# Nine value loads of a decode kernel issued as three partition ranges each

## The chip, the core and the metric

The kernel runs on one NeuronCore of one Trainium2 chip. The metric is the device time of one execution in microseconds (us). All times of the profile come from one profiled execution; "the span" is the time from its first to its last instruction.

## The reference

One decode step of a transformer block with adaptive layer norm, for 8 sequences (one token each) of width 1024:

```python
mod = silu(c) @ w_mod                                # c [8,1024], w_mod [1024, 6*1024]
sa, ca, ga, sb, cb, gb = six parts of mod
h = layernorm(x) * (1 + ca) + sa
x = x + ga * attention(h)                            # 32 query heads, 4 key/value heads of 128
h = layernorm(x) * (1 + cb) + sb
x = x + gb * ((relu(h @ W_gate) * (h @ W_up)) @ W_down)     # width 3584

def attention(h):
    q = h @ wq                                       # [1024, 4096]
    for each sequence b and each key/value head g:   # 8 * 4 = 32 pairs, 8 query heads each
        p = softmax(q @ k_cache[b, g].T / sqrt(128)) # k_cache[b, g]: 8192 x 128, bf16
        o = p @ v_cache[b, g]                        # v_cache[b, g]: 8192 x 128, bf16
    return o @ wo                                    # [4096, 1024]
```

Nearly all bytes are weights and caches that are read once: 64 blocks of keys and values of 2 MB each, and the six weight matrices, 185.6 MB in all.

## The kernel before

**One stream of loads.** Everything that comes from memory passes through one SBUF tensor, `ring` (128 partitions of 11 x 8192 bf16 columns), in a fixed order that the list `stream` holds: 4 blocks of `w_mod` ("mod"), 4 of `A_wq`, then for each of the 32 pairs n a key block ("k", n) and two places later a value block ("v", n), with 4 blocks of `A_wo` in between, then `B_W_gate` and `B_W_up` in turn (4 each), and `B_W_down` in five parts (7, 7, 7, 5 and 2 of 28). There are 89 loads. A key or value block is 8192 columns wide: each of the 128 partitions receives one contiguous piece of 16 KB. A planner written out in the kernel gives each block its place in the ring (`place`) and lists the blocks whose place it takes over (`behind`).

**Who issues and who waits.** All 89 loads are issued by SyncE (line 507 in the profile, engine SP), in the order of `stream`; before each it waits until TensorE has used the blocks that lay there (`users`). Load i signals one of 24 semaphores, i mod 24, and the operation `o` of the load holds the value that tells of its landing (`o.semval`); a semaphore rises by 16 with each transfer. A matmul that reads a block waits for that value. The two small inputs `c` and `x` (8 partitions of 2 KB each) are loaded by ScalarE's queue, and the four parts of the output (8 partitions of 512 B each) leave by SyncE's and ScalarE's queues.

**What the engines do with it.** For pair n, TensorE transposes the key block in 64 tiles (`slot_transpose`, L279 in the profile), VectorE and ScalarE copy them out of PSUM in turn (`slot_evac`, `KT`), and TensorE forms the scores with the transposed tile as its weights. The softmax of pair n-1 (its maximum, the subtraction, Exp) and the product with the values of pair n-2 (`slot_pv`) are woven into the eight steps of pair n. The multiplication with `A_wo` follows by groups of eight pairs. After the attention come the second layer norm, the gate and up products (448 matmuls) and the down product (112 matmuls in five parts, one part for each load of `B_W_down`), two VectorE operations, and the output.

Of the kernel before, what the change touches and what calls it, by code (L numbers as in the profile page):

```python
# [124 lines left out]
def bass_adaLN_cond__gqa_block_cached__glu_gated_reglu__decode_kernel(  # L125
# [30 lines left out]
    NSEM = 24  # L156
# [4 lines left out]
    with ExitStack() as es:  # L161
# [83 lines left out]
        place = {}  # L245
# [3 lines left out]
        for i, (key, cols, src, shape) in enumerate(stream):  # L249
            if at + cols > RING:  # L250
                at = 0
            lo, hi = at, at + cols
            behind.append([k for l, h, k in held if l < hi and h > lo])
            held = [x for x in held if not (x[0] < hi and x[1] > lo)] + [(lo, hi, key)]
            place[key] = ring[:, lo:hi].rearrange("p (k n) -> p k n", n=shape[1])
            at = hi
        loads = {}
        users = {}
        for i, (key, cols, src, shape) in enumerate(stream):
            o = _Op("sp", None, 0)  # L260
            o.sem = rsem[i % NSEM]
            o.semval = 16 * (i // NSEM + 1)
            loads[key] = o

        def pe(fn, reads=(), writes=(), block=None, deps=()):
# [232 lines left out]
        for q in range(4):  # L498
            o = g.dma("sp" if q % 2 == 0 else "act", out.rearrange("b o d -> (b o) d")[:, 256 * q:256 * (q + 1)], outR[32 * q:32 * q + B, :],
                      osem[q], 16, reads=["outR"])  # L500
# [3 lines left out]
        head = []  # L504
        for i, (key, cols, src, shape) in enumerate(stream):
            o = loads[key]
            o.fn = (lambda e, key=key, src=src, o=o: e.dma_start(place[key], src).then_inc(o.sem, 16))  # L507
            o.deps = [users[k] for k in behind[i]]
            head.append(o)
        g.prog["sp"] = head + g.prog["sp"]  # L510
# [40 lines left out]
```

## Time and profile before

| what | value |
|---|---|
| median of 3 runs | 457.0 us (456.96 to 457.01) |
| the profiled execution: its own time | 457.03 us |
| the profiled execution: its span | 455.2 us |
| TensorE busy (PE) | 367.0 us, 81% of the span |
| VectorE busy (DVE) | 175.1 us, 38% |
| ScalarE busy (ACT) | 155.0 us, 34% |
| data moved by SyncE's and ScalarE's queue q1 | 185.61 MB in 17968 packets, 97.3% of the 16 DMA engines' time |
| mean granted TensorE clock | 0.773 of full speed |

PE is TensorE's matmuls, PEld its weight loads, SPq the sequencer of SyncE, on which DMAs are issued. A DMA is carried out by up to 16 DMA engines, each of which moves packets one after the other; in this kernel a packet is one contiguous piece, 16 KB for keys and values. Beside instructions, the trace holds the start, duration, size and queue of each DMA packet (not the number of the engine that moved it), and the time of each landing mark, that is of each step by which a DMA raises its semaphore.

### The profile page before, as it was taken

The numbers are of one execution on the slowest core, as the hardware profiler recorded it, in microseconds if no ns is written. First come the engines' busy times: TensorE is split into PE (matmuls) and PEld (weight loads), VectorE is DVE, ScalarE is ACT, GpSimd is POOL, SyncE is SP. The second block draws the span as 40 slices with busy tenths as digits, with TensorE's granted clock in tenths as the row PEclk, the third lists the DMA queues.
The fourth block names the chain that finished last, engine by engine and source line by source line (L and its number), as shares of the span: only waits on it lengthen the run. The fifth ranks groups of instructions, "written<-read, shape, count | busy, mean of one in ns | idle before, by whom it ended". The sixth has DMA issues, their size and how long they took to land.

```text
span 455.2 us, 16982 instructions
## 1 busy us (share of the span) xinstructions
PE 367.0 (81%) x8008; PEld 353.0 (78%) x8008; DVE 175.1 (38%) x422; ACT 155.0 (34%) x169; POOL 1.5 (0%) x11
## 2 busy tenths in 40 slices
PE   2425487988889999999888698899989999859983
PEld 1425387987888889898888698888889888849971
DVE  1001033455445544445555235544544355530000
ACT  3000045354445434444444234444543344410000
POOL 1000000000000000000000000000000000000000
PEclk9999996598779767768989558967887578855555
DMA  8999999999999999999999999999999999999982
GB/s 348 440 410 421 428 423 430 429 417 426 423 428 422 406 429 424 420 425 429 423 411 416 430 420 426 429 423 417 412 425 425 423 426 400 377 418 420 425 369 112
DMA packets 18101, 186.73 MB, mean 410 GB/s; under 512 B 1472, under 2 KB 1504, under 8 KB 7792
## 3 DMA queue, kind: packets, MB, share of 16 engines
q1 hardware_dynamic: 17968, 185.61, 97.3%
q8 instruction: 62, 1.02, 0.9%
q10 hardware_dynamic: 64, 0.04, 0.0%
q14 instruction: 7, 0.06, 0.0%
HBM read 185.63 MB, written 0.02 MB: 408 GB/s over the span
## 4 chain that ended last, share of the span: by engine, by line
PE 54%; DMA 22%; DVE 12%; SPq 5%; issue 4%; ACT 1%; DVEq 0%
PE PS L279 33%; PE PS L275 21%; DMA ring<-in_A_k_cache_dram 15%; DMA ring<-in_B_W_down_dram 7%; SPq L507 5%; DVE KT L283 5%; DVE mp L283 3%; DVE dg L283 2%; DVE nm L283 1%; ACT KT L286 1%; ACT pt L286 0%; DVE ssub L283 0%; ACT L286 0%; DVE rl L283 0%; DVE outR L283 0%
## 5 line engine op out<-in xcount | busy, mean ns | idle before, releaser
L279 PE MATMUL PS<-identb,ring 128*128 128x128 bf16 x2048 | 199.7, 256 | 7.6 <-DMA ring<-in_A_k_cache_dram 5.5
L286 ACT ACTIVATE KT<-PS 128x1024 bf16<-128x1024 bf16 x128 | 131.0, 1023 | 191.6 <-PE PS L279 170.4
L279 PEld LDWEIGHTS PS<-identb,ring 128*128 128x128 bf16 x2048 | 153.6, 115 | 10.0 <-DMA ring<-in_A_k_cache_dram 6.2
L283 DVE COPY KT<-PS 128x1024 bf16<-128x1024 bf16 x128 | 88.6, 692 | 154.6 <-PE PS L279 153.6
L275 PE MATMUL PS<-qT,KT 128*128 128x8 bf16 x2048 | 94.0, 169 | 0.1
L275 PEld LDWEIGHTS PS<-qT,KT 128*128 128x128 bf16 x2048 | 89.3, 104 | 0.2 <-ACT KT L286 0.2
L275 PE MATMUL PS<-pt,ring 128*128 128x8 bf16 x2048 | 87.9, 167 | 1.3 <-issue 1.2
L275 PEld LDWEIGHTS PS<-pt,ring 128*128 128x128 bf16 x2048 | 71.0, 99 | 1.8 <-issue 1.7
L275 PE MATMUL PS<-dg,ones 8*128 8x8 f32 x64 | 14.1, 290 | 24.9 <-DVE dg L283 24.9
L275 PEld LDWEIGHTS PS<-dg,ones 8*128 8x128 f32 x64 | 11.2, 217 | 27.8 <-DVE dg L283 27.8
L275 PEld LDWEIGHTS PS<-h2T,ring 128*128 128x128 bf16 x448 | 28.5, 162 | 0.4 <-issue 0.4
L275 PE MATMUL PS<-h2T,ring 128*128 128x8 bf16 x448 | 28.5, 204 | 0.0
L275 PE MATMUL PS<-siluT,ring 128*128 128x8 bf16 x384 | 10.9, 168 | 14.6 <-DMA ring<-in_w_mod_dram 14.6
L283 DVE TENSOR_TENSOR ssub<-PS,nb 128x512 f32<-128x512 f32 x32 | 22.1, 692 | 1.2
L275 PEld LDWEIGHTS PS<-siluT,ring 128*128 128x128 bf16 x384 | 10.8, 105 | 14.9 <-DMA ring<-in_w_mod_dram 14.9
L283 DVE TENSOR_REDUCE mp<-PS 128x8 f32<-128x512 f32 x32 | 21.8, 681 | 0.4 <-PE PS L275 0.4
L286 ACT ACTIVATE pt<-ssub 128x512 bf16<-128x512 f32 x32 | 19.9, 622 | 3.5 <-DVE ssub L283 3.5
L275 PE MATMUL PS<-pt,onesb 128*128 128x64 bf16 x256 | 17.1, 225 | 1.7 <-ACT pt L286 1.7
L275 PE MATMUL PS<-hT,ring 128*128 128x8 bf16 x256 | 7.5, 168 | 11.5 <-DMA ring<-in_A_wq_dram 11.5
L275 PEld LDWEIGHTS PS<-hT,ring 128*128 128x128 bf16 x256 | 7.1, 104 | 11.9 <-DMA ring<-in_A_wq_dram 11.9
L286 ACT ACTIVATE qT<-PS 128x256 bf16<-128x256 f32 x1 | 0.4, 383 | 43.7 <-PE PS L275 43.7
L275 PEld LDWEIGHTS PS<-pt,onesb 128*128 128x128 bf16 x256 | 13.0, 117 | 1.9 <-ACT pt L286 1.9
(64 smaller groups left out, 107.0 us busy)
## 6 DMA issues: line engine op xcount, KB each, us to landing
ring<-in_A_k_cache_dram SPq DMA_DIRECT2D x32, 2048.0 KB, 37.2
ring<-in_A_v_cache_dram SPq DMA_DIRECT2D x32, 2048.0 KB, 37.8
ring<-in_w_mod_dram SPq DMA_DIRECT2D x4, 3072.0 KB, 21.4
ring<-in_A_wq_dram SPq DMA_DIRECT2D x4, 2048.0 KB, 42.7
ring<-in_A_wo_dram SPq DMA_DIRECT2D x4, 2048.0 KB, 42.6
ring<-in_B_W_gate_dram SPq DMA_DIRECT2D x4, 1792.0 KB, 28.9
ring<-in_B_W_up_dram SPq DMA_DIRECT2D x4, 1792.0 KB, 27.1
ring<-in_B_W_down_dram SPq DMA_DIRECT2D x3, 1792.0 KB, 29.1
```

The lines of the kernel that those rows point to most:

```text
L275: return pe(lambda e: e.matmul(out_, lhsT, rhs, start=start, stop=stop, skip_group_check=True), reads, writes, block, deps)
L279: return pe(lambda e: e.matmul(out_, in_, ident, start=True, stop=True, is_transpose=True), reads, writes, block)
L283: return g.op("dve", lambda e: getattr(e, name)(*args, **kw), reads, writes)
L286: return g.op("act", lambda e: e.activation(*args, **kw), reads, writes)
L507: o.fn = (lambda e, key=key, src=src, o=o: e.dma_start(place[key], src).then_inc(o.sem, 16))
```

## The change

Nine value blocks, those with n mod 7 equal to 1 or 4 (n = 1, 4, 8, 11, 15, 18, 22, 25, 29), are loaded by three transfers each in place of one: partitions 0 to 111, then 112 to 119, then 120 to 127. The three go out one behind the other on SyncE's queue and raise the same semaphore, by 48 in all, and the values that later loads of that semaphore reach are counted up accordingly. The data, its place in the ring, the order of the stream and the work of the other engines stay as they were; SyncE issues 107 loads in place of 89.

```diff
@@ -254,12 +254,20 @@
+
+        def cuts(key):
+            if key[0] == "v" and key[1] % 7 in (1, 4):
+                return [(0, 112), (112, 120), (120, 128)]
+            return [(0, 128)]
+
         loads = {}
         users = {}
+        landed = [0] * NSEM
         for i, (key, cols, src, shape) in enumerate(stream):
             o = _Op("sp", None, 0)
             o.sem = rsem[i % NSEM]
-            o.semval = 16 * (i // NSEM + 1)
+            landed[i % NSEM] += 16 * len(cuts(key))
+            o.semval = landed[i % NSEM]
             loads[key] = o
@@ -504,7 +512,7 @@
         for i, (key, cols, src, shape) in enumerate(stream):
             o = loads[key]
-            o.fn = (lambda e, key=key, src=src, o=o: e.dma_start(place[key], src).then_inc(o.sem, 16))
+            o.fn = (lambda e, key=key, src=src, o=o: [e.dma_start(place[key][a:z], src[a:z]).then_inc(o.sem, 16) for a, z in cuts(key)])
             o.deps = [users[k] for k in behind[i]]
```

## The prediction

> **What bounds the kernel now.** I read the busy shares first, then the end of the chain of waits, then what TensorE waits for at the end, and last the landing marks of single loads. The page, with shares of the span, 40 slices of DMA, and the queues:
>
> ```profile
> PE 367.0 (81%) x8008; PEld 353.0 (78%) x8008; DVE 175.1 (38%) x422; ACT 155.0 (34%) x169; POOL 1.5 (0%) x11
> ...
> DMA  8999999999999999999999999999999999999982
> ...
> q1 hardware_dynamic: 17968, 185.61, 97.3%
> q8 instruction: 62, 1.02, 0.9%
> ```
>
> No compute engine is full, and the DMA engines are, from the first slice to the last but one. The chain in order of time (start, duration, what), after the attention:
>
> ```profile
> 403.25 1.84 PE PS L275 x64
> ...
> 415.50 2.15 SPq L507
> 417.66 0.04 issue
> 417.70 32.30 DMA ring<-in_B_W_down_dram
> 450.00 0.04 issue
> 450.05 1.87 PE PS L275 x25
> ```
>
> It ends in a load of `B_W_down`. The timeline of TensorE in that stretch, with its idle time and what ended it:
>
> ```profile
> 411.25 28.54 PE L275 MATMUL PS<-h2T,ring 128*128 128x8 bf16 x448
> 440.36 1.66 PE L275 MATMUL PS<-ring,hmT 128*8 128x256 bf16 x28 [0.57 <-DVE hmT L283]
> 442.70 1.66 PE L275 MATMUL PS<-ring,hmT 128*8 128x256 bf16 x28 [0.67 <-DMA ring<-in_B_W_down_dram]
> 446.97 1.67 PE L275 MATMUL PS<-ring,hmT 128*8 128x256 bf16 x28 [2.61 <-DMA ring<-in_B_W_down_dram]
> 450.05 1.83 PE L275 MATMUL PS<-ring,hmT 128*8 128x256 bf16 x28 [1.41 <-DMA ring<-in_B_W_down_dram]
> ```
>
> TensorE has caught up and waits for each part. The last part lands at 451.24, and the span ends 4.0 later. So the end is the last landing plus a fixed tail.
>
> A load has landed when the slowest of its 16 streams (one for each DMA engine) has delivered its eight pieces. The trace's landing marks show that the streams drift apart. The 16 marks of the first `w_mod` block lie within 0.49 us, those of v31 between 381.13 and 392.44 (11.3 us), and those of the last part of `B_W_down` in two groups: eight between 441.38 and 442.45, eight between 449.23 and 451.24. **Eight late streams set the end.**
>
> Why eight are late can be read from the packets. The 62 packets of queue q8 (instructions, 16 KB, 1.07 us each) go to eight streams in turn. Where the first one falls, the stream's next packet starts 0.98 us late and takes 1380 ns in place of 912: 1.45 us lost, and 1.50 at the second. 62 / 8 x 1.5 = 11.6 us, which is the spread of v31.
>
> **Part by part.** *Which streams get more.* The loads of `c` and `x`, 8 partitions each, leave nine marks: one step made at once, and one from each of eight streams. So an 8-partition transfer runs on eight streams with one piece each. A cut load thus puts two pieces on eight streams A, those that serve 8-partition transfers, beside their share of the 112. That share appears in no row. At one end, 112 is split evenly over 16, 7 pieces each: A moves 7 + 1 + 1 = 9 in place of 8, the other eight, B, move 7. At the other end it is 8 pieces on 14 streams: A then moves 10. I take 7, because all 128-piece loads of this trace are split evenly over 16 streams. By the Trainium skill ("DMA: Bandwidth & Descriptors", section on why a DMA increments its semaphore by 16) a transfer uses the largest number of engines up to 16 that divides its partitions, the lowest-numbered ones: 16 for 112, eight for 8. The nine marks agree for 8, no run here shows 112, and the sum would be the same.
>
> *What a piece costs.* Key and value loads land every 4.89 us on an undisturbed stream, 0.611 us per piece. A's streams each get nine pieces more: 9 x 0.611 = +5.5 us, and 18 more completion packets of 6 to 9 ns, +0.1. B's get 9 x 0.611 = 5.5 us less.
>
> *Are late streams in A?* This decides the sign. On a stream, a packet starts 3 to 4 ns before the previous one ends, so streams can be followed from packet to packet. I marked the eight streams that carry a 2 KB piece of `x` (A) and followed all 16. The first two instruction packets (16.34 and 29.91) fall on streams of B, the third and fourth (37.91 and 47.07) on streams of A, each within 1 ns of the place where that stream's next packet was due. From 89.89 on the order repeats on the same streams. And the stream that is last in the first block, 0.54 us behind the first and without a piece of `x`, never gets one and stays in the early group. So the late eight are mixed: at least two of them are in A. Two streams a nanosecond apart can be taken for each other, which is why this is not certain; I give it 9 in 10.
>
> *The sum.* A late stream of A ends 5.6 us later. The two that I identified got eight instruction packets each, like the six marks between 450.7 and 451.24, so if neither of them is the very last, 0.5 us less counts: +5.1 to +5.6, taken as +5.4. The last landing moves from 451.24 to 456.6, and the tail is the same. What B gains is worth nothing, since a load waits for its last stream. The profiled execution took 457.03 (span 455.2 and 1.8 around it), the median of the runs 457.0; so 457.0 + 5.4 = **462.4 us**.
>
> *Costed at nothing.* SyncE issues 18 more DMAs, 0.433 us each at the median, 7.8 us in all. Behind each cut load in its queue stands the next key load. The cover is the backlog of the late streams: the tightest, the first `B_W_up` load, is issued at 387.85 and is begun on the latest stream at 403.56, 15.7 us later. Without that cover each cut load would cost 0.87 us, 7.8 in all. The longest issues (20.6 us for one value load, where the SP queue is held back) come behind `A_wo`; they hold back loads that the late streams reach much later. TensorE waits for one value as before, on the attention's blocks a few us later. It is then ready for the down product at 440.4 and would wait 3.4 us more for its first part; this is the same delay and not a second one.
>
> **Rivals.** *Shorter, because late and B are the same.* Then the late streams lose 5.5 us of work and end at 445.7, and the early ones end at 442.45 + 5.6 = 448.05. The last landing comes 3.2 us sooner: **453.8 us**. TensorE, ready for the down product at 440.36 with 6.8 us of its matmuls to do, would be done at 447.2 and does not prevent it. For it: the two groups are eight and eight, and 9 x 2 x 0.611 = 11.0 us is just the spread. Against it: the packets as followed above. It decides from the point where no late stream carries `x`: 0.09.
>
> *Longer, because pieces collide.* In a 128-piece load each stream writes its own partitions. In a cut load a stream writes partitions that are another's otherwise, and eight streams write 8 neighbouring partitions at once. If two streams that write into the same group of partitions share its way in, each runs at half speed. With one other writer, the 18 extra pieces take 0.611 us more each: 11 us, 473.4 us. With two, 22 us, 484.4; with four, 44 us, 506. Against it: the pieces of `x` went to partitions 0 to 7 while the `w_mod` block was being written there, and all eight took 84 ns, the smallest time of a 2 KB packet of `A_wo`, and no `w_mod` packet beside them lengthened by over 40 ns. They are only 2 KB, and so I leave it 0.24. The Trainium skill ("SBUF — State Buffer", "Door 1: The DMA port swizzle") states that 128 partitions share 16 ports of about 27 GB/s, and by its table 112 to 119 lie on two of them, 120 to 127 on two others. It speaks against this change, and by it four extra writers meet the regular one on a port; a 16 KB piece in 0.611 us is 26.8 GB/s, so an estimate by that page is the last of these cases.
>
> *112 is split over 14 streams.* A gets two pieces more per cut load: +11 us, **468.1 us**; 0.05.
>
> *Nothing moves*, because the cuts end up as one transfer, or the wait at the end is covered by TensorE. Against it: the built kernel's SyncE program does hold the transfers of 112 and of 8 partitions, and TensorE waits 4.7 us for the down blocks: 457.0, 0.02.
>
> **How the numbers follow.** Forecast 0.60, collisions 0.24, 14 streams 0.05, shorter 0.09, nothing 0.02. The likeliest gives 462.4. A change of 0.2%, 0.9 us, is about what a measurement of this kernel can tell from none. Slower: 0.60 + 0.24 + 0.05 = 0.89; faster 0.09; same 0.02. Range: the likeliest case alone is 461.5 to 463.5. Left out at the bottom are the shorter case and no change (0.11); at the top collisions with more than two other writers (0.08): 459 to 484.
>
> **What would show it.** Right: the marks of the last load of `B_W_down` spread over 19 to 21 us in place of 9.9, its last one at about 456.6 on the span's clock, with the packets of a 16 KB piece still at 0.61 us, the cut loads leaving 16 + 9 + 9 marks, and TensorE's waits for the down blocks 3 to 5 us longer. Wrong: a spread under 7 us and an earlier end (late and B are the same); pieces of 1.2 us and more in and behind the cut loads (collisions); an extra delay of 1.2 us per cut load on eight streams with packets at 0.61 (14 streams). If packets, spread and last mark are as forecast but the end is not, the fixed tail was the mistake.

## The result, and the profile after

The changed kernel takes **570.5 us** (median of 4 runs, 564.8 to 571.2) where the kernel before takes 457.0 (456.96 to 457.03): 1.2456 times as long, 95% interval 1.2388 to 1.2524. The direction was the forecast one; the size was not: 113.5 us in place of 5.4, and outside the range of 459 to 484. The profiled execution took 571.2, its span 569.4.

The lines of the page of the changed kernel that answer to those shown of before (busy time and share; DMA and GB/s in 40 slices; the queues):

```profile
PE 404.1 (71%) x8008; PEld 387.2 (68%) x8008; DVE 175.1 (31%) x422; ACT 155.1 (27%) x169; POOL 1.5 (0%) x11
...
DMA  8999999999999999999969999999299999589980
GB/s 365 434 414 425 427 208 410 349 253 423 415 209 364 425 200 292 411 341 211 318 217 344 270 394 425 236 375 387 90 250 389 429 268 376 188 345 419 424 373 20
...
q1 hardware_dynamic: 18112, 185.61, 92.5%
q8 instruction: 62, 1.02, 0.8%
```

(The packets of q1 are SyncE's alone; ScalarE's few went by q10, which the table of before had put under q1.) The same bytes move, and the DMA engines still look full in nearly all slices. But the rate falls to about half wherever a cut load is under way: 208, 253, 209, 200 beside 425. **Busy engines at half the rate mean longer packets, not missing ones.** A stretch between cuts, one around the second cut (v4) and one behind it, from the windows of the changed kernel (the last two columns are DMA share and GB/s):

```profile
90.00:107.00 17.00, 14.16 (x256) 13.99 (x256) 6.37 (x16) 5.04 (x6) 0.00 (x0) 0.52 1.01 425
108.00:125.00 17.00, 12.40 (x244) 11.83 (x242) 5.96 (x15) 5.64 (x6) 0.00 (x0) 0.65 1.02 226
128.00:145.00 17.00, 14.92 (x288) 14.63 (x285) 6.14 (x14) 6.87 (x8) 0.00 (x0) 0.60 1.01 425
```

The first two stretches in the kernel before:

```profile
90.00:107.00 17.00, 15.02 (x358) 14.59 (x356) 9.63 (x24) 8.20 (x9) 0.00 (x0) 0.90 1.01 424
108.00:125.00 17.00, 14.75 (x324) 14.35 (x322) 8.46 (x20) 6.84 (x8) 0.00 (x0) 0.79 1.01 427
```

In the packets of the trace, a 16 KB piece takes 0.61 us between cuts, 0.8 to 1.4 in the 112 partitions of v1 and up to 2.8 at its end, where the two transfers of 8 follow. Over the whole execution their mean rises from 618 to 780 ns.

TensorE's wait for keys is the longest of its DMA waits in the changed kernel's list (us in total, times, longest):

```profile
PEld PS L287 <- DMA ring<-in_A_k_cache_dram: 77.1, 24, 11.4
PE PS L287 <- DMA ring<-in_A_k_cache_dram: 73.1, 22, 11.3
```

The same wait before:

```profile
PEld PS L279 <- DMA ring<-in_A_k_cache_dram: 6.2, 2, 3.6
```

The end itself is unchanged, as the timeline of TensorE shows: it waits for the down blocks just as long as before, only 114 us later.

```profile
556.84 1.67 PE L283 MATMUL PS<-ring,hmT 128*8 128x256 bf16 x28 [0.81 <-DMA ring<-in_B_W_down_dram]
561.12 1.66 PE L283 MATMUL PS<-ring,hmT 128*8 128x256 bf16 x28 [2.61 <-DMA ring<-in_B_W_down_dram]
564.19 1.84 PE L283 MATMUL PS<-ring,hmT 128*8 128x256 bf16 x28 [1.40 <-DMA ring<-in_B_W_down_dram]
```

How much each cut costs can be read from the last landing marks of the loads behind it, against the same loads before: 7.4 us for v1, then 10.7, 11.6, 15.0, 18.9, 12.5, 13.4, 11.8 and 12.8, together 114.1. The last mark of the last load moves from 451.24 to 565.39, which is the same 114.1. From v17 on a single stream is late, where eight were late before: of the 16 marks of k27, fifteen lie within 2.5 us and the last comes 15.3 us after the first.

### The profile page after: what moved, and what is told of

Same layout as the page of the kernel before. It is cut to its first block, busy times and chain, and to the rows that moved or that the text cites. A ratio compares the mean times of both kernels' runs of the same rounds, so it can differ in the third digit from the quotient of the medians.

```text
span 569.4 us, 17000 instructions
## 1 busy us (share of the span) xinstructions
PE 404.1 (71%) x8008; PEld 387.2 (68%) x8008; DVE 175.1 (31%) x422; ACT 155.1 (27%) x169; POOL 1.5 (0%) x11
## 4 chain that ended last, share of the span: by engine, by line
DMA 43%; PE 38%; DVE 6%; another core or an unknown queue 5%; SPq 4%; issue 3%; ACT 0%; DVEq 0%
DMA ring<-in_A_k_cache_dram 31%; PE PS L287 23%; PE PS L283 14%; DMA ring<-in_A_wq_dram 6%; DMA ring<-in_B_W_down_dram 6%; SPq L515 4%; DVE KT L291 3%; DVE mp L291 1%; DVE dg L291 1%; DVE nm L291 1%; DVE ssub L291 0%; DVE stat L291 0%; ACT pt L294 0%; DVE xcT L291 0%
## 5 line engine op out<-in xcount | busy, mean ns | idle before, releaser
L287 PE MATMUL PS<-identb,ring 128*128 128x128 bf16 x2048 | 229.4, 281 | 77.2 <-DMA ring<-in_A_k_cache_dram 73.1
L287 PEld LDWEIGHTS PS<-identb,ring 128*128 128x128 bf16 x2048 | 176.3, 127 | 84.4 <-DMA ring<-in_A_k_cache_dram 77.1
L294 ACT ACTIVATE KT<-PS 128x1024 bf16<-128x1024 bf16 x128 | 131.1, 1024 | 305.0 <-PE PS L287 220.5
L283 PE MATMUL PS<-qT,KT 128*128 128x8 bf16 x2048 | 97.7, 171 | 0.0
L283 PEld LDWEIGHTS PS<-qT,KT 128*128 128x128 bf16 x2048 | 97.0, 109 | 0.0
L283 PEld LDWEIGHTS PS<-pt,ring 128*128 128x128 bf16 x2048 | 72.6, 101 | 7.1 <-issue 7.0
L283 PE MATMUL PS<-dg,ones 8*128 8x8 f32 x64 | 15.8, 317 | 24.7 <-DVE dg L291 24.7
L283 PEld LDWEIGHTS PS<-dg,ones 8*128 8x128 f32 x64 | 12.8, 248 | 27.5 <-DVE dg L291 27.5
L283 PEld LDWEIGHTS PS<-hT,ring 128*128 128x128 bf16 x256 | 7.1, 104 | 11.9 <-DMA ring<-in_A_wq_dram 11.9
```

What stands on the lines that cost most here:

```text
L283: return pe(lambda e: e.matmul(out_, lhsT, rhs, start=start, stop=stop, skip_group_check=True), reads, writes, block, deps)
L287: return pe(lambda e: e.matmul(out_, in_, ident, start=True, stop=True, is_transpose=True), reads, writes, block)
L294: return g.op("act", lambda e: e.activation(*args, **kw), reads, writes)
```

## Experiments

Four theories were open. **W**: streams that write into the same small group of partitions share one way into SBUF (below, a "way"), and a transfer that has not all 128 partitions gives streams other partitions than their usual ones. **S**: the streams meet at the source in memory. **N**: more transfers, marks and issues cost time. **U**: it is the unequal work of the streams, dearer than the sum put it.

**Transfers alone.** A kernel without the computation; each group is issued at once and has landed before the next begins. The thirteen groups, with eight loads each (`rows` takes ranges of partitions; a triple holds the partitions written, the rows read and the columns; `ALL` is all 8192; the comments give the number of the group):

```python
phase(rows((0, 128)))                                       # 1
phase(rows((0, 112), (112, 120), (120, 128)))               # 2
phase(rows((0, 112), (112, 128)))                           # 3
phase(rows((0, 112)))                                       # 4
phase(rows((0, 64), (64, 128)))                             # 5
phase([(slice(0, 128), slice(0, 128), c) for c in ((0, 7168), (7168, 7680), (7680, 8192))])   # 6
phase(rows((112, 120)))                                     # 7
phase([(slice(0, 32, 4), slice(112, 120), ALL)])            # 8
phase([(slice(0, 8), slice(112, 120), ALL)])                # 9
phase([(slice(0, 2), slice(0, 2), ALL)])                    # 10
phase([(slice(0, 8, 4), slice(0, 2), ALL)])                 # 11
phase([(slice(0, 64, 32), slice(0, 2), ALL)])               # 12
phase([(slice(0, 128, 64), slice(0, 2), ALL)])              # 13
```

> Transfers alone: the whole computation is left out, the output is zeros. Thirteen groups of eight loads each, with 16 KB to a partition, on SyncE's queue; a group starts when the one before has landed. In order: 128 partitions whole; 112+8+8; 112+16; 112 alone; 64+64; 128 partitions cut by columns in 7/8, 1/16, 1/16; then transfers of 8 partitions into 112 to 119, into every fourth of 0 to 31, into 0 to 7, all three from the same source rows; then transfers of 2 partitions into 0 and 1, into 0 and 4, into 0 and 32, into 0 and 64, again from the same source rows. Theory W (streams that write into the same small group of partitions share one way in): whole 39 us; by columns 39 to 42; 112+8+8 two to three times as much, 80 to 130, 112+16 and 112 alone well over 45; 64+64 about twice, 75 to 85; eight partitions into 112 to 119 about four times as long as into every fourth (20 against 5 us), the same for 0 to 7; two partitions into 0 and 1 and into 0 and 32 twice as long as into 0 and 4 and 0 and 64 (10 against 5 us), if the groups are those of the prediction's page. Theory S (the streams meet at the source in memory): the three groups of 8 partitions are alike, the four of 2 partitions are alike, 64+64 is like whole. Theory N (the number of transfers and marks costs): by columns is as slow as 112+8+8, and 112 alone takes 7/8 of whole, 34 us.

Windows of this kernel, one for each of the groups 1 to 6, then 7 and 8, then 10 to 13 (the last column, GB/s, counts the time to the landing too):

```profile
0.00:42.80 42.80, 1.15 (x5) 1.00 0.94 392
43.30:124.10 80.80, 0.00 (x0) 1.00 0.90 208
124.60:192.20 67.60, 0.00 (x0) 1.00 0.97 248
192.70:250.20 57.50, 0.00 (x0) 1.00 0.97 255
250.70:332.00 81.30, 0.00 (x0) 1.00 0.98 206
332.60:375.20 42.60, 0.00 (x0) 1.00 0.98 394
375.70:396.60 20.90, 0.00 (x0) 1.00 0.44 50
397.10:404.90 7.80, 0.00 (x0) 1.00 0.38 134
...
426.00:437.30 11.30, 0.00 (x0) 1.00 0.11 23
437.80:445.20 7.40, 0.00 (x0) 1.00 0.10 35
446.00:456.90 10.90, 0.00 (x0) 1.00 0.11 24
457.60:464.90 7.30, 0.00 (x0) 1.00 0.11 36
```

From the first packet to the end of the last, by the trace's packets, with the median packet of 16 KB:

| group | us | GB/s | packet, ns |
|---|---|---|---|
| 1: whole | 40.6 | 413 | 611 |
| 2: 112+8+8 | 79.5 | 211 | 1107 |
| 3: 112+16 | 66.6 | 252 | 1024 |
| 4: 112 alone | 56.6 | 260 | 989 |
| 5: 64+64 | 79.6 | 211 | 1276 |
| 6: by columns | 41.7 | 402 | (14 KB and 1 KB) |
| 7: 8 into 112 to 119 | 19.0 | 55 | 2407 |
| 8: 8 into every fourth of 0 to 31 | 6.5 | 162 | 642 |
| 9: 8 into 0 to 7 | 18.1 | 58 | 2407 |
| 10: 2 into 0 and 1 | 9.9 | 27 | 1292 |
| 11: 2 into 0 and 4 | 6.2 | 42 | 611 |
| 12: 2 into 0 and 32 | 9.4 | 28 | 1225 |
| 13: 2 into 0 and 64 | 6.3 | 42 | 676 |

Groups 7, 8 and 9 read the same source rows with eight streams each, and differ only in the partitions: four streams to a group of four partitions take 2407 ns for a piece, four times the 611 of a stream by itself. Groups 10 to 13 name the sharers: partition 1 and partition 32 share with 0, partitions 4 and 64 do not. **W holds; S and N do not.** (Group 2 took 1.96 times as long as whole loads, just under the two to three times that W had said.) The Trainium skill ("SBUF — State Buffer", section "Door 1: The DMA port swizzle") gives 16 ports of about 27 GB/s, and puts 0 to 3 and 32 to 35 on one, 4 to 7 and 64 to 67 on others. The four pairs agree, with 26.6 and 28.0 GB/s on a shared way; and by its rule a transfer within 64 partitions reaches half the ports, which group 5 agrees with (211 GB/s).

112 partitions alone run at 260 GB/s, where 7/8 of the time of whole loads would have been 35.5 us and not 56.6. Here lies more than half the loss of group 2; the two transfers of 8 add 22.9 us.

**The same loads cut by columns**, in three transfers of 128 partitions (a block has 64 chunks of 128 columns; the rest of the diff is left out):

```diff
-                return [(0, 112), (112, 120), (120, 128)]
-            return [(0, 128)]
+                return [(0, 56), (56, 60), (60, 64)]
+            return [None]
...
-            o.fn = (lambda e, key=key, src=src, o=o: [e.dma_start(place[key][a:z], src[a:z]).then_inc(o.sem, 16) for a, z in cuts(key)])
+            o.fn = (lambda e, key=key, src=src, o=o: [(e.dma_start(place[key], src) if p is None else e.dma_start(place[key][:, p[0]:p[1]], src[:, p[0]:p[1]])).then_inc(o.sem, 16) for p in cuts(key)])
```

> The same nine value loads are three transfers each, but cut by columns: 7/8, 1/16 and 1/16 of each partition's 16 KB, all with 128 partitions. As many transfers and more marks than in the change. Theory W: each stream writes its own partitions as before, so 457 to 459. Theory N (transfers, marks and issues cost): about as slow as the change, 560 to 575. Theory S: the source is read in shorter pieces but from the same rows, 457 to 462.

458.32 us (458.21 to 458.55), ratio 1.0029, interval 1.0018 to 1.0041. As W says. What is left, 1.2 us, is about an estimate from the short pieces: one of 1 KB takes 46 ns in the trace where its share of a 16 KB piece would be 38; 16 of them on each stream in nine loads are 9 x 16 x 8 ns = 1.15 us. So 18 more issues and 288 more marks cost next to nothing.

**112 and 16.**

```diff
-                return [(0, 112), (112, 120), (120, 128)]
+                return [(0, 112), (112, 128)]
```

> The nine loads in two transfers, 112 and 16 partitions. If the 16 go out evenly, one piece to each of 16 streams, every stream has eight pieces again and none gets more work. Theory W: the pieces of the 112 are still written by streams other than the usual ones and the last 16 meet four to a group: most of the loss stays, 530 to 570. Theory U (unequal work, the sum of the prediction, with something that makes it dearer): 457 to 462. Theory T (only the transfers of 8 partitions, eight streams into two groups, are dear): 457 to 475.

553.7 us, in one run. Every transfer leaves 16 marks now, so no stream has more pieces than another, and 96.7 of the 113.5 us are still there: U and T fall. From the list of waits of this kernel:

```profile
PEld PS L287 <- DMA ring<-in_A_k_cache_dram: 54.1, 17, 11.9
```

**One cut load**, at n = 15 and at n = 29:

```diff
-            if key[0] == "v" and key[1] % 7 in (1, 4):
+            if key[0] == "v" and key[1] == 15:       # in the other run: == 29
```

> Only the value load n = 15 is cut into 112+8+8. Theory W with a price per cut load: 113.5/9 = 12.6 us more, 469 to 471. If later cut loads are dearer because the streams are further apart by then: under 467.

> Only the value load n = 29 is cut into 112+8+8, where the streams are 11 us apart; n = 15 alone, with 6 us between them, cost 10.7 us. Theory W1: 10 to 12 us more, 467 to 469. Theory W2 (the distance makes it dear): 13 to 18 us more, 470 to 475.

467.8 and 469.55 us, one run each: 10.7 and 12.5 more. The windows of the kernel with the one cut at n = 15, and of the kernel before, for the same 40 us, show the whole loss in one place:

```profile
200.00:240.00 40.00, 29.47 (x639) 28.52 (x640) 16.97 (x41) 14.38 (x16) 0.00 (x0) 0.75 1.01 304
```

```profile
200.00:240.00 40.00, 35.43 (x836) 34.45 (x834) 21.23 (x49) 18.81 (x21) 0.00 (x0) 0.87 1.01 421
```

304 / 421 of 40 us is 28.9: 11.1 us of transfers are missing. Between the forms of W this pair decides nothing: both times lie between what had been said, 467.8 between "under 467" and 469, 469.55 between 469 and 470.

**One cut among whole loads, alone.** Eight cut loads in a row (not nine, as the text below says) had cost (79.5 - 40.6) / 8 = 4.9 us each, far less than one in the kernel. So the second kernel of transfers alone puts one special load at place 3 of eight:

> Transfers alone again, the computation left out, output zeros. Nine groups of eight value or key loads, all whole except the one at place 3: (1) whole too; (2) 112+8+8; (3) 112+16; (4) only the 112, the last 16 partitions left out; (5) only the two transfers of 8, the 112 left out; (6) whole, and two transfers of 8 into every fourth of partitions 0 to 31, which by theory W are the usual ones of the eight streams that serve them; (7) whole, and two such transfers into every fourth of 64 to 95, usual ones of other streams; (8) as (1), behind eight transfers of 8 into partitions of the first kind, so that eight streams start 4.9 us behind the others; (9) as (2), behind the same eight. Question: nine cut loads in a row cost 4.9 us each (79.5 against 40.6 us for eight), one cut among whole loads in the kernel 10.7. Theory W1 (a displaced stream always takes from a way that its owner needs, so a cut between whole loads is dearer than one between cut ones): (2) is 8 to 11 us over (1). Theory W2 (it is the distance between the streams that makes it dear): (2) about 5 over (1), and (9) over (8) clearly more, 8 to 12. (6) is 1.2 over (1), (7) 2.5 to 5 over (1) by W in either form; if only the amount of work on a stream counted, (6) and (7) would be alike at 1.2. (8) is 4.9 over (1).

| group | us | over the group it is compared with |
|---|---|---|
| 1: whole | 40.6 | |
| 2: one 112+8+8 | 47.2 | +6.6 over 1 |
| 3: one 112+16 | 45.1 | +4.6 |
| 4: one 112 alone | 42.9 | +2.3, with 0.6 us less to move |
| 5: one pair of 8 alone | 41.3 | |
| 6: whole, and two of 8 into every fourth of 0 to 31 | 41.7 | +1.1 |
| 7: whole, and two of 8 into every fourth of 64 to 95 | 43.4 | +2.8 |
| 8: as 1, behind eight transfers of 8 | 47.6 | +7.0 over 1 |
| 9: as 2, behind eight transfers of 8 | 56.6 | +9.0 over 8 |

The windows of groups 1, 2 and 7 of this kernel, and of 8 and 9 (last column GB/s, with the time to the landing):

```profile
0.00:42.80 42.80, 1.15 (x5) 1.00 0.94 392
43.30:91.50 48.20, 0.00 (x0) 1.00 0.96 348
...
268.70:313.10 44.40, 0.00 (x0) 1.00 0.96 384
313.60:362.60 49.00, 0.00 (x0) 1.00 0.88 364
363.10:421.10 58.00, 0.00 (x0) 1.00 0.86 307
```

Neither form of W had the size right: a single cut with the streams together costs 6.6, more than the 5 of W2 and less than the 8 of W1. And groups 8 and 9 did not hold eight streams back by 4.9 us. SyncE took 5.3 us to issue the eight transfers of 8, and the other eight streams began only then. The marks of the first whole load lie within 2.7 us in group 8 and 3.0 in group 9 (a single stream is last by 1.0 and 1.8 us), against 0.6 to 0.7 in groups 1 and 2. The late start of the others is also why group 8 took 7.0 us more than group 1, and not 4.9.

So group 9 tells what a cut costs that is met with the streams 3.0 us apart: 9.0. Put in order of the distance in the last load before the cut, the costs are 6.6 (0.6 us apart, group 2), 7.4 (1.9, v1 of the changed kernel), 9.0 (3.0), 10.7 (3.6, v4), 10.7 (6.3, n = 15 alone) and 12.5 (11.2, n = 29 alone). Each is from one run. **Up to there, a cut is dearer the further apart the streams are, or at least not cheaper.** In the changed kernel the cost rises from v8 over v11 to v15 as well (11.6, 15.0 and 18.9 at 6.4, 10.7 and 15.3 us), faster than in the kernels with a single cut; but the last four cuts, met with the streams 15 to 22 us apart, cost only 11.8 to 13.4. So the distance alone does not give the cost.

Why distance makes a cut dear was argued and not tried. An estimate: apart, a stream pays for its own 9 displaced pieces that meet an owner, and at another time for 8 displaced pieces of others that pass over its way, 17 x 0.611 = 10.4, and 0.6 for its additional piece: 11.0, against 10.7 and 12.5 measured. It takes all nine pieces as displaced, which no run shows, and does not give the 15.0 and 18.9; these stay open. The transfers alone leave a part open too: nine cuts at 6.6 to 9.0 us would be 59 to 81 of the 114 us.

**Additional pieces without any cut.** Two kernels keep all loads whole and add eight small transfers, which move 5632 bytes into each of 8 partitions of a tile that nobody reads:

```diff
+            if key[0] == "v" and key[1] in (1, 4, 8, 11, 15, 18, 22, 25):
+                m = (1, 4, 8, 11, 15, 18, 22, 25).index(key[1])
+                p0 = 0 + m % 4 + 32 * (m // 4)          # in the other run: 64 + ...
+                extra = [(scr[p0:p0 + 29:4, :], A_v_cache[0, 0].rearrange("(p c) d -> p (c d)", p=128)[112:120, 0:2816])]
```

> The kernel before, unchanged but for eight additional transfers of 8 partitions, 5632 bytes each, right behind the value loads 1, 4, 8, 11, 15, 18, 22 and 25, into an own small tile that nobody reads, at every fourth partition of 0 to 63: by theory W the usual partitions of the eight streams that serve them. It asks whether there are late streams among those eight (the sign in the prediction) and whether a piece costs what the sum put. If so: 8 x 0.21 = 1.7 us more, 458.2 to 458.9. If the late streams are all among the other eight: 457.1 to 457.4.

> As the run with additional transfers, the same streams and bytes, but into every fourth partition of 64 to 127, the usual partitions of the other eight streams. If only the amount of work on a stream counts: the same time as that run. Theory W: each additional piece shares its way with the stream that owns it, so it takes twice as long and slows the owner too, 1.7 to 5 us more than that run.

Into the usual partitions of the streams that carry them: 458.45 us (457.09 to 458.78), ratio 1.0028, interval 1.0016 to 1.0040. Four of six runs lie 1.4 to 1.8 us above the 457.0 of before, about the sum (1.7 us); two lie at 457.1, as if nothing had been added. The trace is of one of these two, and it shows how that can be. Of the eight pieces behind v25, six start between 328.22 and 331.26 and two at 336.08 and 336.31: two of the eight streams are among the late ones. And the late marks of the last load now lie between 450.68 and 451.30, where before two of the eight lay at 449.23 and 449.28. If those were the two streams, they took 1.7 us without becoming the last. That the four slower runs had two others there is not shown.

Into others' partitions: 459.91 us (459.86 to 461.15), ratio 1.0069, interval 1.0057 to 1.0082. The same streams, bytes and number of transfers cost twice as much, 2.9 against 1.4 us, because of the partitions alone. The difference, 1.5 us, is just under the 1.7 to 5 that W had said. The trace (of the run of 461.15) shows that mostly the owners pay: an additional piece takes 215 to 294 ns where it took 215 to 222 in the other kernel, not twice as long, but the mean of the 16 KB packets rises to 623.2 ns from 617.7, which it was before and in the other kernel. That is 44.7 us over all streams, more than the 13.9 us of the additional pieces themselves; why so much is open.

## Why the prediction was wrong

**What bounds the kernel** held in the main: the end is the last landing and a fixed tail, and both landing and end moved by the same 114 us. But in the changed kernel one late stream sets the end, not eight.

**Which streams get more, and whether late ones are among them** held as far as it was tried. A cut load leaves 16 + 9 + 9 marks: 112 partitions run on 16 streams and each 8 on eight, so the rival of 14 streams is out. In the run with additional pieces two of the eight streams are among the late ones, as the prediction had read from its packets, and four of its six runs became slower by about the whole sum. That puts the rival on the faster side wrong too. So the price of a piece that goes to a stream's usual partitions was right; it is not what this change mostly does. That the time went the way that was forecast is therefore no merit of the sum: with no additional piece on any stream (112+16) most of the loss was there.

**What a piece costs is the step that failed.** The sum took 0.611 us for a piece, whichever stream writes it into whichever partition. The trace of before had only loads of 128 partitions, in which every stream writes its usual ones, and the figure was carried over to loads in which it does not. With two streams on one way a piece takes 1.2 to 1.3 us, with four 2.4 (groups 10, 12, 7 and 9), and the mean 16 KB packet of the changed kernel rose from 618 to 780 ns.

**The rival "pieces collide" was the case, and mis-sized twice.** It had 0.24 where it was nearly all. First, it was priced for the 18 extra pieces of eight streams alone; the 7 pieces of the 112 on all 16 streams were left at nothing, and 112+16 shows that they and the last 16 make 96.7 of the 113.5 us. Second, it left out the whole loads beside a cut, whose owners are slowed too. The worst figure it gave, 506 with four other writers on the extra pieces, was 49 us over the kernel before, and the range ended at 484, just short of its own case of two (484.4). What spoke against it, the pieces of `x` at 84 ns beside the running `w_mod` load, was not worth what was put on it: eight pieces of 2 KB whose starts lie 0.01 to 0.4 us apart, so that few of them ran side by side. Why they left no mark on the `w_mod` packets was not tried. The page of the Trainium skill that spoke against the change ("SBUF — State Buffer", section "Door 1: The DMA port swizzle") was right here: its figure for a way, about 27 GB/s, agrees with the 26.6 and 28.0 of groups 10 and 12.

**Costed at nothing**: SyncE's issues did not stay what they were. The list of one line's instructions (duration minimum, median and maximum in ns) shows a value transfer that held SyncE for 41.2 us; the second row is from the kernel before:

```profile
L515 SPq DMA_DIRECT2D ring<-in_A_v_cache_dram x50: 295/1077/41232, 34.2 to 456.7; - x50
L507 SPq DMA_DIRECT2D ring<-in_A_v_cache_dram x32: 327/433/20623, 34.1 to 353.2; - x32
```

This goes with the one late stream: while an issue is held, streams that are ahead run out of loads, and the DMA share falls (slices of 2 and 5 in the page above). Around 408 us the packets of a single stream are left, but from the first load to the last there is no moment without a packet under way. So the last stream seems to have had work all the time; then this is not where the 114 us come from.

**What would show it**: of the signs of the forecast, only the 16 + 9 + 9 marks came. The last load's marks spread over 11.9 us in place of 19 to 21, and the waits for the down blocks did not grow. Packets of 1.2 us and more in the cut loads and beside them were the sign that the text had named for collisions.

No version here beats the kernel before. The DMA engines are busy 97% of the time there, so a piece that one stream takes over from another is not gained: it meets the owner of the way it goes to.

## What to carry to other kernels

Where loads run at the full rate, look at which partitions each stream writes, not only at how many bytes: here transfers of 112, 64 or 8 neighbouring partitions sent streams over each other's ways, and a cut load slowed the loads beside it too, while 8 partitions four apart (every fourth of 0 to 31) did neither. A load that has to be cut is better cut by columns, which cost 1.2 us for nine loads in place of 113.5. A piece's time from a profile holds only for transfers of the same shape; before it is used for another shape, measure that shape by itself. And a rival that a page of the Trainium skill gives with figures should be priced with all the pieces that it would touch, before a small contrary row is set against it.

## What was not expected of the hardware

Partitions 0 and 32 share a way and 0 and 64 do not (28.0 and 41.6 GB/s for two streams). The eight late streams come from 62 instruction packets of 16 KB that fall on eight streams in turn; the two that were measured took 1.45 and 1.50 us from their stream. And the mean granted TensorE clock was lower in the changed kernel, 0.656 against 0.773 before in the profiled executions, with TensorE busy for 71% of the span against 81%; no run here shows why. Nothing here shows that the clock set the time.
